# Winograd's form of Strassen's scheme for the last product of a two-layer expert network

## The chip, the cores and the metric

The kernel runs as one program on one core of a Trainium2 chip. Its time is the device time of one execution in microseconds; a comparison uses the median of several. Of the kernel before there are three runs: 1787.97, 1789.3 and 1793.09 us, median 1789.3. The engines are TensorE (PE; its weight loads are shown as PEld), VectorE (DVE), ScalarE (ACT), GpSimd (POOL) and SyncE (SP), whose queue issues all the transfers.

## The reference

Chunked attention, then two gated or activated expert layers on 4608 tokens of 512 numbers; everything is float32.

```python
scores = scale * np.matmul(q_c, k_c.transpose(0, 1, 2, 4, 3))      # chunks of 64
attn = softmax(scores)
x = np.matmul(attn, v_c)  # -> 4608 x 512
g = x @ w_gate;  x = (g * sigmoid(g) * (x @ w_val)) @ w_out        # layer 1, d_ff = 1536
h = x @ w_in                                                       # layer 2, d_ff = 2048
out = (h * sigmoid(1.702 * h)) @ w_out2
```

## The kernel before

A float32 product is done as three matmuls of the type fp32r: each operand is split into a high part (a cast on ScalarE or GpSimd) and a low part (a subtraction), and `mm3` (line 243) adds hi x hi, hi x lo and lo x hi in PSUM. `split` (line 239) makes the two parts.

The tokens are cut into 9 blocks of 512, the columns of a layer into tiles of 128. `passes` (line 252) has two passes per layer; a pass keeps its input weights in SBUF (the ring `w`, 21 tiles of 512 KB) and runs over all 9 blocks. A pass of the first layer has three groups of two column tiles of each of its two matrices, a pass of the second layer two groups of four column tiles.

The input products already use Winograd's form of Strassen's scheme: for each group `group_products` (line 526) computes seven products of 256 x 256 x 256 instead of eight, each of 12 matmuls with 256 columns, from seven combinations of the weights (`combos`, line 331, made ahead by `group_to_dram` and kept in DRAM as `wd_`) and seven of the tokens (`token_combos`, line 482, made by `x_to_dram` for the second layer). Two PSUM banks take them in turn, `ga` and `gb` or `s` and `a`; ScalarE and VectorE put the four quarters of the result together. `gated` (line 563) makes the activation h and its two parts.

The last product of a group is plain: `second` (line 582) multiplies the parts of h by an output weight tile (`od_`, loaded for each block in a ring `o` of three) into four sums of 512 columns, `ya` and `yb`, two banks each. These output steps (three matmuls of 512 columns; 16 per group in the second layer) are kept in the list `pend` and put between the products of the following group by `put` (line 690). `block_sum` (line 598) adds the sums of a pass: in the first pass of a layer they go to DRAM, in the last they are loaded again, added and, in the second layer, stored to the output.

All instructions are collected as operations with an engine, an estimated duration and a priority (`Program.op`, line 76), and `emit` (line 99) writes them out in the order of a planned run: at each step the engine that is free first takes the operation of lowest priority number among those that can begin. So each engine's order is fixed before the program runs. `spread` (line 664) puts the preparation of the next pass's weights (reading the 64-bit host words, combining, splitting, storing) over the pass before; GpSimd does the combining and splitting, with a ring `ws` of two tiles whose stores must land before a tile is used again.

## Time and profile before

| | |
|---|---|
| median of 3 runs | 1789.3 us |
| profiled execution | 1787.97 us, its span 1786.2 us |
| PE busy | 1736.1 us, 97% of the span, 13096 matmuls |
| DVE busy | 1068.7 us, 60% |
| ACT busy | 796.0 us, 45% |
| POOL busy | 489.9 us, 27% |
| DMA | 473.50 MB, 265 GB/s on average |
| PE on the chain that ended last | 90% of the span |

Busy time counts an engine as busy from the start to the end of each of its instructions; successive matmuls overlap in it, so a busy PE says only that matmuls follow closely, and the distance from one start to the next says how fast they run. The table is for the whole span; the stages differ and are read from stretches of it.

### The profile page before, as it was taken

What the parts mean: (1) busy time and instruction counts of PE and PEld (TensorE: products, weight loads), DVE (VectorE), ACT (ScalarE), POOL (GpSimd) and SP (SyncE); (2) the same over time, 40 slices, a digit from 0 to 9 for tenths busy, and PEclk for the clock granted to TensorE, in tenths of its full rate; (3) what the DMA queues carried; (4) which work ended last, traced back from release to release, by engine and by line L of the source; (5) the groups of instructions that cost most, each with busy time, mean ns of one, the idle gap of its engine ahead of it and who ended that gap; (6) DMA issues with size and microseconds to landing.
All of it is one profiled execution on the core that took longest, in us unless ns stands there. A gap on an engine that the chain in (4) does not pass through costs nothing.

```text
span 1786.2 us, 33210 instructions
## 1 busy us (share of the span) xinstructions
PE 1736.1 (97%) x13096; PEld 1579.0 (88%) x13096; DVE 1068.7 (60%) x1628; ACT 796.0 (45%) x1392; POOL 489.9 (27%) x542
## 2 busy tenths in 40 slices
PE   7779999999999999999999999999999999999998
PEld 6769998989899999999999998888888898888886
DVE  6787788778875467667666665333334444444444
ACT  5767666666663344444443354333333332322222
POOL 4664555455623144443353231000000000000000
PEclk8889999999999999999999999999999999999999
DMA  6567887788769988998889999766668666666664
GB/s 254 177 208 270 273 289 250 249 298 283 250 223 350 333 292 300 312 318 305 293 293 337 350 349 346 254 212 218 215 215 295 232 235 228 234 226 227 233 220 158
DMA packets 183915, 473.50 MB, mean 265 GB/s; under 512 B 19792, under 2 KB 46416, under 8 KB 183760
## 3 DMA queue, kind: packets, MB, share of 16 engines
q1 hardware_dynamic: 183760, 471.38, 76.4%
q8 instruction: 104, 1.70, 0.4%
q14 instruction: 51, 0.42, 0.1%
HBM read 336.56 MB, written 134.74 MB: 264 GB/s over the span
## 4 chain that ended last, share of the span: by engine, by line
PE 90%; DVE 4%; ACT 1%; issue 1%; POOL 0%; DMA 0%; DVEq 0%; ACTq 0%; SPq 0%; POOLq 0%
PE yb L244 6%; PE ya L245 6%; PE ya L244 6%; PE ya L246 6%; PE yb L246 6%; PE yb L245 6%; PE ga L244 6%; PE ga L246 6%; PE ga L245 6%; PE gb L244 4%; PE gb L246 4%; PE gb L245 4%; PE s L245 3%; PE s L246 3%; PE s L244 3%; PE a L246 2%
## 5 line engine op out<-in xcount | busy, mean ns | idle before, releaser
L237 DVE TENSOR_TENSOR h<-h,c 128x512 f32<-128x512 f32 x360 | 271.5, 768 | 39.2 <-ACT h L571 35.8
L244 PE MATMUL ga<-x,w 128*128 128x256 f32 x944 | 272.2, 288 | 19.1 <-ACT u L228 11.6
L571 ACT ACTIVATE h<-c 128x512 f32<-128x512 f32 x252 | 156.6, 632 | 274.9 <-DVE c L237 264.3
L246 PE MATMUL ga<-x,w 128*128 128x256 f32 x944 | 268.3, 284 | 0.7 <-POOL w L237 0.7
L245 PE MATMUL ga<-x,w 128*128 128x256 f32 x944 | 267.9, 284 | 0.0
L237 DVE TENSOR_TENSOR hl<-h,hh 128x512 fp32r<-128x512 f32 x252 | 187.6, 751 | 68.5 <-ACT hh L228 65.0
L228 ACT CAST hh<-h 128x512 fp32r<-128x512 f32 x252 | 155.8, 620 | 121.2 <-DVE h L237 72.8
L228 ACT COPY u<-ga 128x512 f32<-128x512 f32 x177 | 103.5, 585 | 235.5 <-PE ga L246 235.1
L237 DVE TENSOR_TENSOR c<-u,gb 128x512 f32<-128x512 f32 x177 | 121.0, 684 | 142.9 <-ACT u L228 107.4
L244 PEld LDWEIGHTS ga<-x,w 128*128 128x128 f32 x944 | 179.6, 190 | 29.4 <-ACT u L228 13.0
L244 PE MATMUL gb<-x,w 128*128 128x256 f32 x708 | 202.3, 286 | 0.0
L245 PE MATMUL gb<-x,w 128*128 128x256 f32 x708 | 201.0, 284 | 0.4 <-POOL x L237 0.4
L246 PE MATMUL gb<-x,w 128*128 128x256 f32 x708 | 201.3, 284 | 0.0
L245 PEld LDWEIGHTS ga<-x,w 128*128 128x128 f32 x944 | 179.9, 191 | 6.7
L246 PEld LDWEIGHTS ga<-x,w 128*128 128x128 f32 x944 | 179.8, 191 | 1.2 <-POOL w L237 1.2
L246 PE MATMUL s<-x,w 128*128 128x256 f32 x496 | 139.8, 282 | 0.0
L245 PE MATMUL s<-x,w 128*128 128x256 f32 x496 | 139.5, 281 | 0.0
L244 PE MATMUL s<-x,w 128*128 128x256 f32 x496 | 139.2, 281 | 0.0
L245 PEld LDWEIGHTS gb<-x,w 128*128 128x128 f32 x708 | 135.2, 191 | 4.0 <-POOL x L237 0.6
L244 PEld LDWEIGHTS gb<-x,w 128*128 128x128 f32 x708 | 135.2, 191 | 3.9
L246 PEld LDWEIGHTS gb<-x,w 128*128 128x128 f32 x708 | 135.1, 191 | 0.0
L237 DVE TENSOR_TENSOR c<-u,a 128x512 f32<-128x512 f32 x93 | 63.6, 684 | 117.7 <-ACT u L228 109.9
(144 smaller groups left out, 4223.8 us busy)
## 6 DMA issues: line engine op xcount, KB each, us to landing
x<-x_dram SPq DMA_DIRECT2D x189, 512.0 KB, 5.6
o<-od_b SPq DMA_DIRECT2D x144, 512.0 KB, 4.9
o<-od_a SPq DMA_DIRECT2D x102, 512.0 KB, 5.4
x_dram<-x SPq DMA_DIRECT2D x63, 512.0 KB, 4.6
wd_b<-ws SPq DMA_DIRECT2D x56, 256.0 KB, 5.2
w<-wd_b SPq DMA_DIRECT2D x28, 512.0 KB, 7.0
raw<-in_moe_w_out SPq DMA_DIRECT2D x56, 255.8 KB, 5.2
wd_a<-ws SPq DMA_DIRECT2D x42, 256.0 KB, 4.6
```

The costliest lines, as they stand in the source:

```text
L228: op("act", act_us(n), lambda: nc.scalar.copy(out=dst.ap, in_=cut(src.ap)), [src], [dst], prio)
L237: lambda: e.tensor_tensor(out=dst.ap, in0=of_a(a.ap), in1=of_b(b.ap), op=by), [a, b], [dst], prio)
L244: nc.tensor.matmul(o, ah, bh, start=first, stop=False, **kind)
L245: nc.tensor.matmul(o, ah, bl, start=False, stop=False, **kind)
L246: nc.tensor.matmul(o, al, bh, start=False, stop=last, **kind)
L571: op("act", act_us(512), lambda h=h, i=i, var=var, by=by: nc.scalar.activation(out=h.ap, in_=of(var)(c[i].ap), func=AF.Sigmoid, scale=by), ...
```

## The change

The second layer's last product is also computed with seven products instead of eight: the four quarters of a group's h (two halves of the columns, two halves of the tokens) are combined to seven operands, and so are the output weights. `group_gated` replaces `group_products` and `gated` for that layer: its seven input products all go into the bank `ga` in turn (some of them accumulate there), each is read by a copy or an add, and the gates and the seven operands follow, the operands in tiles of rings that the attention used. `last_product` is an output step for one of the seven labels and one half: six matmuls of 256 columns. The seven sums of a block stand in the seven other banks until `o_sum` combines them to four quarters. `out_combos` makes seven combinations of the output weights in the pass before; those of the first group stay in SBUF for a pass (`WO`, in the ring `w`), those of the second are loaded for each block. `x_to_dram` uses more buffers for the last block. In the first group of the layer three of the products have banks of their own. In the planner a product may follow its reader after 0.25 us (`near`), and a step of TensorE that depends on another follows it at once.

The core of the diff; a line of dots marks what is left out.

```diff
                     late = (0.3, 1.2)[a.eng == "pe" and o.eng != "pe"] + (1.5 if o.eng == "dma" else 0.0)
-                    a.done_at = max(a.done_at, end + (0.13 if a.eng == o.eng else late))
+                    if a.near and o.eng != "dma":
+                        late = 0.25
+                    a.done_at = max(a.done_at, end + ((0.0 if a.eng == "pe" else 0.13) if a.eng == o.eng else late))
...
+    GV, YS, OS = 1.42, 0.70, 0.714
+    ORDER = {1: "1265743", 2: "1675243", "o": "1245673"}
+    def step_us(g):
+        return 7 * GV + (4 * YS * len(g.fs) if g.layer == 1 else 14 * OS)
...
+        def of_pair(kind, tiles, made, name, done, order, var):
+            def fn(prio):
+                t0, t1 = [conv_tile((g.name, kind, var, i), tiles[i], prio) for i in range(2)]
+                for j, (m, src, cut) in enumerate(made(t0, t1, prio)):
+                    s = ring["ws"].new([P, 2, 256], F32R)
+                    hi, lo = [s.part(lambda ap, c=c: ap[:, c]) for c in range(2)]
+                    split(hi, lo, src, 256, prio + j, "pool", cut, "pool")
+                    i = order.index(m)
+                    store(done[i][0][:, i, var], s, [done[i][1].part(None)], prio + j)
...
+        if passes[p][0] == 2:
+            WO[gs[0]] = seven_load("w", gs[0], OD, [prio + (1 + i / 7) * step - 15 for i in range(7)])
...
+        for n, (m, src, cut) in enumerate(token_combos(xb, prio)):
+            i = ORDER[2].index(m)
+            pairs = ["qk", "ve"] if b < NB - 1 else ["qk", "ve", "tt", ("raw", "raw"), ("ws", "ws"), "hh", "te"]
+            hi, lo = [ring[t].new([P, 2, HT], F32R) for t in pairs[n % len(pairs)]]
+            split(hi, lo, src, 512, prio + n, "pool" if b < NB - 1 else ("dve", "pool")[n % 2], cut)
...
+    def group_gated(g, xs, at, put, early):
+        s1, u2, u3 = [ring["u"].new([P, 2, HT]) for _ in range(3)]
+        made = {}
+        hs = []
...
+        def gate(c, k, prio):
+            if not hs:
+                hs.append(ring["xr"].new([P, 4, 2, HT]))
+            h = hs[0].part(lambda ap: ap[:, k])
+            op("act", act_us(512), lambda: nc.scalar.activation(out=h.ap, in_=c.ap, func=AF.Sigmoid, scale=1.702),
+               [c], [h], prio, "sig")
+            tt(h, h, c, ALU.mult, 512, prio)
+            return h
+        def parts(label, src, prio, eng="dve"):
+            made[label] = [ring[t].new([P, 2, HT], F32R) for t in HOMES[label]]
+            split(*made[label], src, 512, prio, eng)
+        def follow(label, prio):
+            m = bank[label]
+            if label == "1":
+                copy(s1, m, 512, prio)
+            elif label == "6":
+                copy(u2, m, 512, prio)
+            elif label == "7":
+                copy(u3, m, 512, prio)
+                tt(u2, u2, u3, ALU.subtract, 512, prio, "pool")
+            elif label == "5":
+                c = quarter()
+                copy(c, m, 512, prio)
+                tt(u2, u2, c, ALU.add, 512, prio, "pool")
+                a["22"] = gate(c, 3, prio + 1)
+                parts("4", a["22"], prio + 3, "pool")
+            elif label == "2":
+                c = quarter()
+                tt(c, s1, m, ALU.add, 512, prio)
+                a["11"] = gate(c, 0, prio + 1)
+                parts("1", a["11"], prio + 2)
+            elif label == "4":
+                c = quarter()
+                tt(c, u3, m, ALU.subtract, 512, prio)
+                a["12"] = gate(c, 1, prio + 1)
+                parts("2", a["12"], prio + 3)
+            else:
+                c = quarter()
+                tt(c, u2, m, ALU.add, 512, prio)
+                a["21"] = gate(c, 2, prio + 1)
+        a = {}
+        alone = {"2": "gb", "3": "s", "4": "a"} if early else {}
+        z = ring["ga"].new([P, 2, HT])
+        bank = {label: ring[alone[label]].new([P, 2, HT]) if label in alone else z for label in ORDER[2]}
+        for i, label in enumerate("1263745" if early else ORDER[2]):
+            n = ORDER[2].index(label)
+            product(bank[label], W[g][n], xs[n], label in "675", at(i), True)
+            if label != "3" or not early:
+                follow(label, at(i))
+            if i == 6:
+                if early:
+                    follow("3", at(i))
+                prio = at(i)
+                tt(a["22"], a["21"], a["22"], ALU.add, 512, prio + 1)
+                parts("5", a["22"], prio + 2)
+                tt(a["21"], a["11"], a["21"], ALU.subtract, 512, prio + 2)
+                tt(a["11"], a["22"], a["11"], ALU.subtract, 512, prio + 2)
+                parts("6", a["11"], prio + 3)
+                parts("7", a["21"], prio + 4)
+                tt(a["12"], a["12"], a["11"], ALU.subtract, 512, prio + 4)
+                parts("3", a["12"], prio + 5)
+            put(i)
+        return made
...
+    def last_product(bank, label, w, parts, var, first, last, prio):
+        hi, lo = parts
         def fn():
-            if layer == 1:
-                mm3(ys[e].ap, w.ap[:, 0, es], w.ap[:, 1, es], hh.ap, hl.ap, first, last)
+            for t in range(2):
+                ts = slice(t * P, (t + 1) * P)
+                mm3(bank.ap[:, t], hi.ap[:, var, ts], lo.ap[:, var, ts], w.ap[:, var, 0], w.ap[:, var, 1],
+                    first and t == 0, last, skip_group_check=True)
+        op("pe", OS, fn, [w, hi, lo], [bank], prio)
...
+    def o_banks():
+        ya, yb = [ring["y" + i].new([P, 2, 2, 256]) for i in "ab"]
+        one = [ring[t].new([P, 2, 256]) for t in ("gb", "s", "a")]
+        two = [t.part(lambda ap, i=i: ap[:, i]) for t in (ya, yb) for i in range(2)]
+        return dict(zip("1245673", two + one))
...
+        m = banks[label]
+        if label == "1":
+            kept["s"] = ring["e"].new([P, 2, 256])
+            copy(kept["s"], m, 512, prio)
+        elif label == "2":
+            c = part_of(0, "yv")
+            if final:
+                tt(c, c, kept["s"], ALU.add, 512, prio, "pool")
+                tt(c, c, m, ALU.add, 512, prio)
+            else:
+                tt(c, kept["s"], m, ALU.add, 512, prio)
+            out_quarter(0, c)
+        elif label == "6":
+            tt(kept["s"], kept["s"], m, ALU.add, 512, prio)
+        elif label == "7":
+            u2, u3 = kept["s"], ring["e"].new([P, 2, 256])
+            tt(u3, u2, m, ALU.add, 512, prio)
+            c = part_of(3, "yv")
+            if final:
+                tt(c, c, u3, ALU.add, 512, prio, "pool")
+                tt(c, c, banks["5"], ALU.add, 512, prio)
+            else:
+                tt(c, u3, banks["5"], ALU.add, 512, prio)
+            out_quarter(3, c)
+            tt(u3, u3, banks["4"], ALU.subtract, 512, prio)
+            if final:
+                c = part_of(2, "t")
+                tt(c, c, u3, ALU.add, 512, prio, "pool")
+                u3 = c
+            out_quarter(2, u3)
+            tt(u2, u2, banks["5"], ALU.add, 512, prio)
+        elif label == "3":
+            u4 = kept["s"]
+            tt(u4, u4, m, ALU.add, 512, prio)
+            if final:
+                c = part_of(1, "t")
+                tt(c, c, u4, ALU.add, 512, prio, "pool")
+                u4 = c
+            out_quarter(1, u4)
...
+                after_first = p and passes[p - 1][0] < layer and b == j == 0
+                def put(i, tj=tj, n=n, step=step, layer=layer, after_first=after_first):
+                    left = n * (7 - i - (i > 3)) // 8 if layer == 1 else 0 if after_first else n * (6 - i) // 7
+                    while len(pend) > left:
+                        pend.pop(0)(tj + (i + (i > 4) + 0.5 + (n - len(pend) if after_first else 0)) * step / 8)
...
```

## Rows read from the trace of the kernel before

**Rows 1.** Stretches: PE, PEld, DVE, ACT, POOL busy us (instructions), PEclk, DMA share, GB/s.

```profile
0.00:545.00 545.00, 504.35 (x5098) 458.42 (x5099) 432.08 (x674) 353.77 (x612) 287.93 (x329) 0.96 0.74 253
545.00:1013.00 468.00, 467.30 (x3242) 435.17 (x3241) 301.91 (x440) 190.13 (x342) 175.61 (x182) 1.00 0.91 315
1013.00:1393.00 380.00, 380.00 (x2387) 341.66 (x2386) 171.15 (x263) 137.08 (x241) 26.35 (x32) 1.00 0.77 264
1393.00:1777.00 384.00, 384.00 (x2375) 343.71 (x2374) 161.84 (x251) 115.05 (x199) 0.00 (x0) 1.00 0.64 223
sum 1786.20, PE 1736.12 PEld 1579.01 DVE 1068.67 ACT 796.03 POOL 489.89; mean PE 347.22 PEld 315.80 DVE 213.73 ACT 159.21 POOL 97.98
```

**Rows 2.** Timeline of TensorE in the second layer: start, duration, instruction.

```profile
1203.94 0.28 PE L244 MATMUL gb<-x,w 128*128 128x256 f32 x1
...
1205.36 0.39 PE L244 MATMUL yb<-o,hh 128*128 128x512 f32 x1
...
1206.76 0.28 PE L244 MATMUL ga<-x,w 128*128 128x256 f32 x1
```

**Rows 3.** Timeline of VectorE: the same instruction in two successive blocks.

```profile
1459.69 0.69 DVE L237 TENSOR_TENSOR c<-u,gb 128x512 f32<-128x512 f32 x1 [3.50 <-ACT u L228]
...
1501.99 0.69 DVE L237 TENSOR_TENSOR c<-u,gb 128x512 f32<-128x512 f32 x1 [3.47 <-ACT u L228]
```

**Rows 4.** Timelines of TensorE, ScalarE and VectorE around hand-offs of a bank.

```profile
1201.05 0.28 PE L246 MATMUL ga<-x,w 128*128 128x256 f32 x1
1201.37 0.59 ACT L228 COPY u<-ga 128x512 f32<-128x512 f32 x1 [2.03 <-PE ga L246]
...
128.45 0.67 DVE L237 TENSOR_TENSOR c<-u,ga 128x512 f32<-128x512 f32 x1
129.18 0.39 PE L244 MATMUL ga<-x,w 128*128 128x256 f32 x1 [0.97 <-DVE c L237]
```

**Rows 5.** Groups of instructions, 1400 to 1750 us: count, busy, mean ns, idle before.

```profile
L237 DVE TENSOR_TENSOR h<-h,c 128x512 f32<-128x512 f32 x68 | 46.1, 687 | 11.6 <-ACT h L571 10.8
...
L237 DVE TENSOR_TENSOR c<-u,gb 128x512 f32<-128x512 f32 x25 | 17.2, 689 | 41.0 <-ACT u L228 31.0 <-PE gb L246 10.0
```

**Rows 6.** The same groups, 1000 to 1100 us, GpSimd at work.

```profile
L237 DVE TENSOR_TENSOR h<-h,c 128x512 f32<-128x512 f32 x24 | 18.6, 789 | 3.3 <-ACT h L571 3.2
...
L237 DVE TENSOR_TENSOR c<-u,gb 128x512 f32<-128x512 f32 x8 | 5.5, 684 | 8.2 <-ACT u L228 5.3 <-ACT raw L321 2.8
```

**Rows 7.** Timelines of VectorE and GpSimd: the first layer's last block.

```profile
1031.44 0.69 DVE L237 TENSOR_TENSOR xr<-yv,yb 128x512 f32<-128x512 f32 x1 [0.30 <-DMA yv<-y_dram]
...
1056.69 1.29 POOL L237 TENSOR_TENSOR k<-xr,q 128x512 fp32r<-128x512 f32 x1 [4.31 <-DMA x_dram<-k]
```

**Rows 8.** Stretches of full and of steady transfers.

```profile
1060.00:1130.00 70.00, 70.00 (x437) 62.72 (x436) 34.22 (x55) 28.18 (x52) 12.31 (x20) 1.00 0.98 348
1400.00:1750.00 350.00, 350.00 (x2191) 314.42 (x2190) 150.99 (x234) 107.36 (x186) 0.00 (x0) 1.00 0.66 232
```

**Rows 9.** Timeline of GpSimd: a cast that waited for a store, its subtraction.

```profile
1082.37 0.40 POOL L230 CAST ws<-t 128x256 fp32r<-128x256 f32 x1 [7.87 <-DMA od_b<-ws]
1082.85 0.74 POOL L237 TENSOR_TENSOR ws<-t,ws 128x256 fp32r<-128x256 f32 x1
```

**Rows 10.** Timelines at the end: TensorE, VectorE, the queue of SP.

```profile
1777.09 0.39 PE L246 MATMUL yb<-o,hl 128*128 128x512 f32 x1
...
1781.72 1.28 DVE L237 TENSOR_TENSOR yv<-yv,yb 128x512 f32<-128x512 f32 x2 [4.31 <-DMA yv<-o_dram]
1782.44 0.93 SPq L224 DMA_DIRECT2D out<-yv  x2
```

**Rows 11.** Timeline of TensorE after a long idle time.

```profile
72.41 0.58 PE L244 MATMUL ga<-x,w 128*128 128x256 f32 x1 [4.42 <-ACT u L228]
```

**Rows 12.** Stretches behind that idle time.

```profile
72.40:75.00 2.60, 2.59 (x12) 2.60 (x13) 2.60 (x4) 1.90 (x5) 2.60 (x3) 0.50 0.53 199
75.00:79.00 4.00, 4.00 (x14) 3.23 (x14) 3.89 (x7) 3.96 (x6) 1.78 (x2) 0.59 0.19 44
```

More of the change, by code (lines that the diff above doesn't have):

```diff
@@ L66 @@
 class Op:
-    __slots__ = ("eng", "us", "fn", "prio", "deps", "follows", "table", "n", "done_at")
+    __slots__ = ("eng", "us", "fn", "prio", "deps", "follows", "table", "near", "n", "done_at")
 class Program:
@@ L280, in attention_two_moe_kernel @@
             start[p].append(t)
-            t += sum(7 * GV + 4 * YS * len(g.fs) for g in gs) + (13.0 if p == 0 and b < NB - 1 else 0)
+            t += sum(step_us(g) for g in gs) + (13.0 if p == 0 and b < NB - 1 else 0)
     start.append([t])
@@ L534, in group_products @@
         for i, (k, goes_on) in enumerate(((0, 0), (1, 0), (0, 1), (1, 0), (0, 1), (0, 0), (1, 1))):
[L535 to L546 removed]
+            m, at_i = bank[k], at(i)
+            product(m, W[g][i], xs[i], goes_on, at_i)
             if i == 0:
@@ new lines, in attention_two_moe_kernel, with quarter @@
+    HOMES = {"1": ("hh", "hl"), "2": ("hh", "hl"), "4": ("hh", "hl"), "5": ("h", "h"), "6": ("q", "k"), "7": ("v", "xt"),
+             "3": ("xt", "xt")}
+    def group_gated(g, xs, at, put, early):
+        s1, u2, u3 = [ring["u"].new([P, 2, HT]) for _ in range(3)]
+        made = {}
+        hs = []
+        quarters = []
+        def quarter():
+            if not quarters:
+                c = ring["c"].new([P, 2, 2, HT])
+                quarters.extend(c.part(lambda ap, k=k: ap[:, k]) for k in range(2))
+            return quarters.pop(0)
+        def gate(c, k, prio):
[60 more added lines that the diff above has]
+            put(i)
+        return made
@@ L594, in attention_two_moe_kernel @@
     y_dram = pool["dram"].tile([P, KD, NT], F32, name="y_dram")
-    o_dram = pool["dram"].tile([P, KD, NT], F32, name="o_dram")
+    o_dram = pool["dram"].tile([P, NB, 4, 512], F32, name="o_dram")
+    od2 = {}
     yd = {}
     def block_sum(p, b, ys, e, prio):
-        layer = passes[p][0]
-        first = p == 0 or passes[p - 1][0] != layer
-        last = p == NPASS - 1 or passes[p + 1][0] != layer
-        dram = (y_dram if layer == 1 else o_dram)[:, e, b * BT:(b + 1) * BT]
-        if first:
-            s = ring["yv"].new([P, BT])
+        dram = y_dram[:, e, b * BT:(b + 1) * BT]
+        s = ring["yv"].new([P, BT])
+        if p == 0:
@@ L606, in block_sum @@
             copy(s, ys[e], 512, prio, "act" if e % 2 else "dve")
-            yd[layer, b, e] = Buf(None)
-            store(dram, s, [yd[layer, b, e]], prio)
+            yd[b, e] = Buf(None)
+            store(dram, s, [yd[b, e]], prio)
             return
-        s = ring["yv"].new([P, BT])
-        load(s, dram, prio - 14, [yd[layer, b, e]])
-        if last and layer == 1:
-            if e == 0:
-                xr[b] = ring["xr"].new([P, KD, BT])
-            tt(xr[b].part(lambda ap: ap[:, e]), s, ys[e], ALU.add, 512, prio)
-            if e == KD - 1:
-                x_to_dram(xr.pop(b), b, prio + 3)
-            return
@@ L619, in block_sum @@
-        tt(s, s, ys[e], ALU.add, 512, prio)
-        if last:
-            t0 = b * BT + e * P
-            store(out[t0:t0 + P, :], s, [], prio)
-        else:
-            yd[layer, b, e] = Buf(None)
-            store(dram, s, [yd[layer, b, e]], prio)
+        load(s, dram, prio - 14, [yd[b, e]])
+        if e == 0:
+            xr[b] = ring["xr"].new([P, KD, BT])
+        tt(xr[b].part(lambda ap: ap[:, e]), s, ys[e], ALU.add, 512, prio)
+        if e == KD - 1:
+            x_to_dram(xr.pop(b), b, prio + 3)
@@ L683, in attention_two_moe_kernel @@
             xs = X.pop((p, b))
[L684 removed]
             for j, g in enumerate(gs):
[L686 removed]
+                step = step_us(g)
                 tj = t + j * step
                 n = len(pend)
[L690 to L715 removed]
```

216 lines of the change are left out of this document (128 added, 88 removed).

## The prediction

> **What bounds the kernel now.** The page's busy line comes first: TensorE is busy for 1736 of 1786 us, VectorE for 1069. That is an average over stages, so the next view is the table of stretches. It shows the attention stage with the first pass of the first layer (to about 545 us, TensorE idle for 40 us of it), the second pass (0.7 us idle), the two passes of the second layer (busy 380.00 of 380 and 384.00 of 384 us), and then a tail of 9.2 us in which TensorE has stopped [rows 1]. The change touches the second layer, and there nothing ends a wait of TensorE, so only three things can change the time: the length of TensorE's own stream, new waits in it, and the tail. That the busy time is dense work and not overlapping records is seen in the timeline: inside a product of 12 matmuls of 256 columns one starts every 0.118 us (1203.94 to 1205.36, 1.42 us for 12), and six matmuls of 512 columns follow one another in 1.40 us, 0.233 us each [rows 2]. The granted clock is 1.00, which is the 2.4 GHz level [rows 1].
>
> One group of four column tiles is then 7 products of 12 short matmuls and 16 output steps of 3 long ones: 84 x 0.118 + 48 x 0.233 = 9.94 + 11.20 = 21.14 us; a block of two groups should take 42.28. The same VectorE instruction returns after 42.30 us in successive blocks [rows 3]. So the stage is accounted for without a gap.
>
> **TensorE's stream.** The 48 long matmuls of a group become 7 labels x 2 halves x 2 token tiles x 3 = 84 short ones. At the spacing of the products, which also load a weight tile for each matmul, they take 84 x 0.118 = 9.94 us. The group loses 1.26 us, and 36 groups (two passes, nine blocks, two groups) lose **45.4 us**. The bounds on that are narrow, since the shape (128x256, its own weight load) is the one already measured: with the planner's own 0.714 us for six matmuls it would be 43.3.
>
> **The hand-off of the one product bank.** Today the products alternate between banks. Now all seven of a group go through one bank, so each waits until ScalarE or VectorE has read the one before. Rows on both sides of that hand-off exist. ScalarE starts its copy 0.32 us after the start of the last matmul (1201.05 to 1201.37), and the copy takes 0.59 us; VectorE's add from PSUM takes 0.67 to 0.69; TensorE, when it waits for one, starts 0.06 us after its end (128.45 + 0.67 to 129.18) [rows 4, 5]. From the start of the last matmul to the next product that is 0.97 us by ScalarE and 1.07 by VectorE, if VectorE starts as soon as ScalarE does. The two output steps queued between two products cover 1.42 us plus the matmul's own 0.12, so 0.6 and 0.5 us are left over. An uncovered hand-off costs 0.85 us (0.97 less the 0.12 that the next matmul would have taken anyway).
>
> What can use up the slack is work in front of the reader. Per group ScalarE now has 15 instructions of about 0.6 us (9 of 20 us) and VectorE 17; with the seven of the block's sums 41 per block, spaced 0.61 us where two follow each other (two in 1.28) [rows 10]: 25 of 39.8 us, 63% instead of 43% [rows 8]. An instruction that has just begun holds the reader for at most 0.6 us, which the slack nearly covers. Beside GpSimd VectorE is slower: in 1000 to 1100 us, with GpSimd at work, h<-h,c took 789 ns, against 687 later without it, while the add from PSUM (c<-u,gb) kept 684 against 689 [rows 5, 6]. The new kernel gives GpSimd three instructions of 512 elements, 1.3 us each [rows 7], in every group, so this comes back in part. I take 0.1 us per group, **+4 us** (between 0 and 0.5 per group, 18 us).
>
> By the Trainium skill (Perfetto Trace Analysis, Optimizing Tensor Performance) independent matmul groups should rotate through different PSUM banks, and larger matmuls are more efficient than smaller ones. Both speak against this change. On the second half the rows agree only faintly: 256 columns cost 0.118 us in the short form and 0.117 in the long. The first half, taken at its worst, is the second rival below.
>
> **First boundary, at about 1013 us.** The gates of the second layer now write a tile of the ring xr, which has one buffer, and the last block of the first layer holds that buffer until x_to_dram has split it. Before, its last sum came at 1031.44, its last split on GpSimd at 1056.69, after 4.31 us of waiting for a store [rows 7]: 26 us for the splitting. The new buffer pairs of the last block take these store waits away, and every other split goes to VectorE; four sums and four splits at 0.6 are some 5 us. In that time TensorE has the second group's products, but no output steps to put between them: four hand-offs at 0.85 are 3.4 us, and some 3 more until the first parts are made. I take **+6 us**; 0 if the sums come earlier, 20 if the buffer is freed as late as today.
>
> **Second boundary, at about 1370 us.** Of the 21 buffers w the second layer used 14; now the first group's seven output weights stay in the other seven, and nothing of the next pass can be loaded until the last block frees them. Around the boundary, in some 60 us, 21 weight tiles, 14 input tiles and 7 output tiles of 512 KB and 2 MB of sums must pass: 24 MB, 400 GB/s. The rows show 348 GB/s at a DMA share of 0.98, and 232 at 0.66 in steady state [rows 8]. 24 MB at 348 GB/s take 69 us, so up to 9 us are missing; I take **+4 us** (0 to 9).
>
> **What hides.** Making the output weights takes GpSimd, per group, 6 more pairs of a cast (0.40) and a subtraction (0.74) and 8 more sums of about 0.74 us [rows 9]: 13 us, 26 per pass, in stretches where it is busy for 176 of 468 us and for 26 of 380; in the last pass it has nothing left to do [rows 1], so the work was ready well ahead. Output weights loaded: 8 tiles per block before, 7 now. If this cover goes, GpSimd's queue is what is late (third rival). In the first layer only the planner's constant for a step that follows another on TensorE changes; its second pass has 0.7 us to lose or win, and I put the reordering at 0 (up to 5 us either way).
>
> **The tail.** TensorE's last matmul starts at 1777.09; then two loads of old sums wait for their buffers, VectorE adds at 1781.72, the last stores are issued from 1782.44, and the span ends at 1786.2, 9.1 us later [rows 10]. Afterwards the four old quarters have four buffers, so the loads are done early, and behind the last matmul stand 0.4 us to the reader, an add on VectorE (0.69), one on GpSimd (1.3) and a store as now (3.3 from the second store's issue to the end, the two issues taking 0.93): 5.7. **-3 us** (between -5 and 0). The gate chain of the last group ends about 8.5 us after its last product by durations of 0.6 to 0.7 us an instruction, and the output steps ahead of its last label last 10, so it should not wait there.
>
> **Sum.** The profiled execution took 1788.0 us (span 1786.2): 1788.0 - 45.4 + 4 + 6 + 4 - 3 = 1753.6. The median of the runs is 1.3 us above the profiled one, so **1755 us**.
>
> **Rivals.**
> 1. *No new wait*: only the stream and the tail count. 1788.0 - 45.4 - 3 + 1.3 = 1741. For it: the slack of the hand-off and the planner's order. Against it: both boundaries lack a buffer.
> 2. *The gain turns into bubbles at the one bank.* 252 products at 0.85 us each would be 214 us and a kernel at 1955. By the Trainium skill's rule on rotating banks, above, it would go this way. The slack of 0.5 us speaks against it; but if 41 of the 252 are uncovered (one in six), the gain of 34 us is gone and the time stays near 1789.
> 3. *GpSimd's queue*, the slower side. Today TensorE needs nothing from GpSimd in the second layer. Now the adds that make u2, and a part of a22, stand in its queue behind the weight preparation for the next pass, and its casts wait for stores: 7.87 us before the one at 1082.37, the longest such wait of that stretch [rows 9]. From the fourth product to the read of the seventh are three slots of 2.85 us, less a copy and an add of 2 us: 6.5 us of slack. A hold of 7.9 us costs 1.4 us and the reader behind it a hand-off of 0.85; with the 56 stores of one pass, at 1.2 us each on average, 67 us, less what is saved: 1822. It decides from 0.6 us per store on. Against it: the long holds came where GpSimd had little else to do, and DMA was full (0.98) only until 1130 us [rows 8].
> 4. *The clock.* After 4.42 us of idle [rows 11] TensorE's clock was 0.50 (the 1.2 GHz level) from 72.4 to 75 us and 0.59 for 4 us more [rows 12]: half of 2.6 and 0.41 of 4 are 2.9 us lost. Twelve such drops would eat the gain; one in each group costs 104 us, 1859 us. Bubbles of 0.85 us are far below that idle time, and in the first 545 us, with 40 us of idle in it, the mean clock was still 0.96 [rows 1]. The Trainium skill (TensorE: Matmul & The Clock Gate, "A second HAM failure mode") does tell of a kernel that cycles PSUM banks and loses its clock to frequent small idles. No stretch of the second layer shows it yet.
>
> **Chances.** The forecast, with waits somewhat below or far above my 14 us (1746 to 1784): 0.67. The first rival 0.15, the second 0.07, the third 0.08, the fourth 0.03. About 0.3% (5 us) is what a measurement of this kernel tells from no change. Faster: 0.67 + 0.15 = 0.82; within 0.3%: 0.07; slower: 0.11. From 1741 to 1784 lie the forecast and nearly all of the first rival, 0.8.
>
> **What would show it.** In the new profile the block period in the second layer should be near 40 us (42.30 now), with 168 short matmuls per group at 0.118 us and no bubble before most products; VectorE near 63% there; gaps of TensorE only at the two boundaries, a few us each; about 6 us behind the last matmul. It is wrong if gaps stand before products in every block with ScalarE or VectorE as releaser (second rival), if VectorE's add for the last product waits for GpSimd (third), or if the clock of a second-layer stretch is below 1.00 (fourth).

## The result, and the profile after

The changed kernel takes 1806.4 us (median of four, 1805.4 to 1806.7) against 1789.5 us of the kernel before on the same chip: ratio 1.0091, 95% interval 1.0073 to 1.0108. It is slower by 17 us, where 34 us less were forecast. The table of stretches, with the columns of [rows 1], cut at 545, 1013 and 1393 us as there:

```profile
545.00:1013.00 468.00, 467.77 (x3243) 435.52 (x3242) 272.09 (x396) 167.49 (x296) 135.66 (x131) 1.00 0.84 291
1013.00:1393.00 380.00, 357.59 (x2853) 348.55 (x2852) 306.96 (x425) 191.06 (x338) 189.42 (x199) 0.98 0.85 286
1393.00:1797.00 404.00, 391.68 (x3218) 384.47 (x3217) 286.28 (x394) 174.54 (x294) 123.99 (x91) 1.00 0.72 233
```

The first layer is as it was (its last output step starts at 1028.7, before at 1027.7). In the second layer TensorE, which had no idle time in [rows 1], is idle for 22 us of 380 and for 12 of 404. VectorE has 306.96 us of work there in place of 171, GpSimd 189 in place of 26.

The stream itself did become shorter. VectorE's timeline, the same instruction in successive blocks, twice late in the layer's first pass (pass 1) and twice in its last pass:

```profile
1322.39 0.69 DVE L241 TENSOR_TENSOR c<-u,ga 128x512 f32<-128x512 f32 x1 [0.56 <-PE ga L250]
...
1363.17 0.69 DVE L241 TENSOR_TENSOR c<-u,ga 128x512 f32<-128x512 f32 x1 [0.56 <-PE ga L250]
...
1444.70 0.69 DVE L241 TENSOR_TENSOR c<-u,ga 128x512 f32<-128x512 f32 x1 [0.56 <-PE ga L250]
...
1486.65 0.69 DVE L241 TENSOR_TENSOR c<-u,ga 128x512 f32<-128x512 f32 x1 [0.56 <-PE ga L250]
```

The block takes 40.78 us in the one and 41.95 in the other; it took 42.30 [rows 3]. Taking from TensorE's timeline every distance between matmul starts beyond 0.1185 us gives the waits (with what half clock adds to the distances): 0.8 us in a quiet block of pass 1, 2.1 in one of the last pass, none in the kernel before. From the last output step of layer 1 on, the first six stretches up to that VectorE instruction in successive blocks (to 1281 us) hold 8.8, 13.6, 5.0, 2.4, 2.4 and 3.5 us, and the end of the stream 4.3. The list of TensorE's waits (engine, line and releaser: us, times, longest), 1028 to 1055 us, and then 1055 to 1108:

```profile
PE ga L248 <- ACT u L232: 2.1, 3, 0.7
PE ga L248 <- DVE c L241: 1.8, 1, 1.8
PE ya L248 <- ACT hh L232: 1.7, 1, 1.7
PE ga L248 <- ACT c L232: 0.7, 1, 0.7
PE ya L250 <- DVE hl L241: 0.5, 1, 0.5
```

```profile
PE ga L248 <- ACT u L232: 3.1, 2, 1.9
PE yb L248 <- DMA o<-od_b: 1.7, 1, 1.7
PE ga L248 <- DVE c L241: 1.6, 2, 1.2
PE ya L248 <- ACT hh L232: 0.7, 1, 0.7
```

In the second list a hand-off is late by up to 1.9 us, not by the bare 0.85: the reader itself began late. And there the clock fell. Stretches of the same columns:

```profile
1028.00:1055.00 27.00, 20.20 (x151) 18.51 (x150) 20.94 (x29) 13.58 (x26) 11.17 (x7) 1.00 0.96 353
1055.00:1062.00 7.00, 5.17 (x42) 4.79 (x41) 4.50 (x7) 3.78 (x7) 4.28 (x5) 1.00 0.99 334
1062.00:1070.00 8.00, 7.32 (x38) 6.80 (x37) 7.00 (x11) 4.79 (x11) 4.64 (x5) 0.57 0.84 314
1070.00:1075.00 5.00, 2.69 (x21) 2.27 (x19) 5.00 (x6) 3.43 (x7) 3.46 (x4) 1.00 0.72 228
1075.00:1080.00 5.00, 4.22 (x22) 4.22 (x23) 2.85 (x6) 2.37 (x5) 4.04 (x6) 0.66 0.72 238
...
1123.00:1128.00 5.00, 5.00 (x32) 5.00 (x31) 3.58 (x5) 2.30 (x4) 2.67 (x3) 0.66 0.60 215
```

TensorE had been busy for 20.2 of 27 and 5.2 of 7 us when the mean fell to 0.57, near the 1.2 GHz level. Ahead of the third fall it had waited 2.2 us for one copy (to 1122.51). By the means 0.43 x 8 + 0.34 x 5 + 0.34 x 5 = 6.8 us at most went there; the distances between matmul starts that grew from 0.12 to 0.21 us add up to 5.2.

The preparation of the last pass's weights is in another place. Stores of prepared weights in the kernel before, 750 to 1010 us and 1010 to 1300 us (count, KB, median us to landing):

```profile
wd_b<-ws SPq DMA_DIRECT2D x18, 256.0 KB, 5.5
od_b<-ws SPq DMA_DIRECT2D x8, 256.0 KB, 6.7
...
od_b<-ws SPq DMA_DIRECT2D x8, 256.0 KB, 5.8
wd_b<-ws SPq DMA_DIRECT2D x6, 256.0 KB, 6.1
```

and in the changed one:

```profile
od_b<-ws SPq DMA_DIRECT2D x2, 256.0 KB, 5.8
...
wd_b<-ws SPq DMA_DIRECT2D x28, 256.0 KB, 4.6
od_b<-ws SPq DMA_DIRECT2D x28, 256.0 KB, 4.4
```

All 56 stores of a pass now fall behind 1010 us. The split of the first layer's last block takes tiles of the rings t, raw and ws; the preparation needs the same rings and is written later in the program, so in the planned order it stands behind that split.

In the last pass the timeline shows most of what makes a block 1.2 us longer than in pass 1 (GpSimd, VectorE, ScalarE, TensorE):

```profile
1512.53 3.39 POOL L241 TENSOR_TENSOR t<-t,e 128x512 f32<-128x512 f32 x2 [2.03 <-DVE e L241]
1512.98 0.68 DVE L241 TENSOR_TENSOR e<-e,a 128x512 f32<-128x512 f32 x1
1513.57 3.63 DVE L241 TENSOR_TENSOR xr<-xr 128x512 f32<-128x512 f32 x3
1516.51 0.62 ACT L232 CAST v<-xr 128x512 fp32r<-128x512 f32 x1 [1.09 <-DVE xr L241]
1517.23 0.62 ACT L232 CAST q<-xr 128x512 fp32r<-128x512 f32 x1
1517.76 0.58 ACT L232 COPY u<-ga 128x512 f32<-128x512 f32 x1
1518.39 0.38 PE L248 MATMUL ga<-x,w 128*128 128x256 f32 x1 [0.55 <-ACT u L232]
```

While GpSimd makes its two final adds, three VectorE instructions take 1.21 us each (0.69 in e1, where VectorE makes those adds); the casts wait for them, and the copy of the product bank stands behind the casts in ScalarE's fixed order.

The tail: TensorE's last matmul starts at 1797.67, the span ends at 1803.6, 5.9 us later.

### The profile page after: what moved, and what is told of

Read it like the earlier page. It is cut to its first block, busy times and chain, and to the rows that moved or that the text cites. A ratio compares the mean times of both kernels' runs of the same rounds, so it can differ in the third digit from the quotient of the medians.

```text
span 1803.6 us, 36622 instructions
## 1 busy us (share of the span) xinstructions
PE 1718.8 (95%) x14392; PEld 1623.1 (90%) x14392; DVE 1302.3 (72%) x1884; ACT 883.6 (49%) x1536; POOL 751.5 (42%) x762
## 4 chain that ended last, share of the span: by engine, by line
PE 72%; DVE 14%; issue 3%; ACT 3%; DMA 2%; POOL 1%; SPq 0%; POOLq 0%; DVEq 0%; ACTq 0%
PE ga L248 9%; PE ga L250 8%; PE ga L249 8%; DVE xr L241 4%; PE yb L248 4%; PE gb L248 4%; PE yb L250 4%; PE yb L249 4%; PE gb L250 4%; PE gb L249 4%; PE ya L249 3%; PE ya L248 3%; PE ya L250 3%; PE s L248 2%; PE s L250 2%
## 5 line engine op out<-in xcount | busy, mean ns | idle before, releaser
L248 PE MATMUL ga<-x,w 128*128 128x256 f32 x1652 | 480.1, 291 | 44.3 <-ACT u L232 29.7
L250 PE MATMUL ga<-x,w 128*128 128x256 f32 x1652 | 468.2, 283 | 1.0 <-POOL w L241 1.0
L249 PE MATMUL ga<-x,w 128*128 128x256 f32 x1652 | 467.4, 283 | 0.0
L248 PEld LDWEIGHTS ga<-x,w 128*128 128x128 f32 x1652 | 313.8, 190 | 65.3 <-ACT u L232 37.9
L249 PEld LDWEIGHTS ga<-x,w 128*128 128x128 f32 x1652 | 314.0, 190 | 4.1
L250 PEld LDWEIGHTS ga<-x,w 128*128 128x128 f32 x1652 | 313.9, 190 | 1.5 <-POOL w L241 1.5
L241 DVE TENSOR_TENSOR xr<-xr,c 128x512 f32<-128x512 f32 x144 | 129.6, 902 | 103.9 <-ACT xr L650 99.8
L241 DVE TENSOR_TENSOR h<-h,c 128x512 f32<-128x512 f32 x216 | 167.6, 792 | 12.6 <-ACT h L612 10.9
L241 DVE TENSOR_TENSOR c<-u,ga 128x512 f32<-128x512 f32 x146 | 99.9, 684 | 68.0 <-PE ga L250 66.2
L248 PE MATMUL gb<-x,w 128*128 128x256 f32 x496 | 143.0, 288 | 1.1 <-DVE c L241 1.1
L249 PE MATMUL gb<-x,w 128*128 128x256 f32 x496 | 141.4, 285 | 1.1 <-POOL x L241 1.1
L250 PE MATMUL gb<-x,w 128*128 128x256 f32 x496 | 141.7, 286 | 0.0
L612 ACT ACTIVATE h<-c 128x512 f32<-128x512 f32 x108 | 68.2, 633 | 121.1 <-DVE c L241 120.7
L241 DVE TENSOR_TENSOR xr<-xr 128x512 f32<-128x512 f32 x144 | 118.9, 825 | 4.2 <-POOL hl L241 0.6
L650 ACT ACTIVATE xr<-c 128x512 f32<-128x512 f32 x144 | 90.7, 632 | 58.3 <-DVE c L241 52.7
L241 POOL TENSOR_TENSOR k<-xr,q 128x512 fp32r<-128x512 f32 x24 | 41.4, 1724 | 156.6 <-DVE xt L241 89.4
L248 PEld LDWEIGHTS gb<-x,w 128*128 128x128 f32 x496 | 95.3, 192 | 4.2 <-DVE c L241 1.3
```

What stands on the lines that cost most here:

```text
L241: lambda: e.tensor_tensor(out=dst.ap, in0=of_a(a.ap), in1=of_b(b.ap), op=by), [a, b], [dst], prio)
L248: nc.tensor.matmul(o, ah, bh, start=first, stop=False, **kind)
L249: nc.tensor.matmul(o, ah, bl, start=False, stop=False, **kind)
L250: nc.tensor.matmul(o, al, bh, start=False, stop=last, **kind)
L612: op("act", act_us(512), lambda h=h, i=i: nc.scalar.activation(out=h.ap, in_=of(0)(c[i].ap), func=AF.Sigmoid), [c[i]], [h], prio, "sig")
L650: op("act", act_us(512), lambda: nc.scalar.activation(out=h.ap, in_=c.ap, func=AF.Sigmoid, scale=1.702), [c], [h], prio, "sig")
```

## The experiments

Time from layer 1's last output step to TensorE's last matmul, from each profile: before 749.4 us, changed 769.0. It is given with each run, since layer 1 itself ended between 1025.9 and 1036.7 us in these profiles (below). It is one profile each time: up to 1390 us e1 has the changed kernel's order of instructions on every engine, yet its first six stretches hold 33.0 us of waits where the changed kernel's hold 35.7, so up to 3 us there say nothing. The first eight runs have one execution each, beside the kernel before at 1788.5 (e1 to e4) and 1790.5 us (e5, e6, e7, e9).

**e1_final_dve.** The four final adds of the last pass go from GpSimd to VectorE.

```diff
-                tt(c, c, kept["s"], ALU.add, 512, prio, "pool")
+                tt(c, c, kept["s"], ALU.add, 512, prio)
...
```

> The four adds of old sums that each block of the last pass gives to GpSimd go to VectorE; nothing else is changed. Theory A (GpSimd's reads hold VectorE's sums of two SBUF tiles, the casts behind them stand in ScalarE's queue in front of the copy of the product bank, and TensorE waits for that copy): the block of the last pass falls from 42.0 to about 40.8 us, as in the end of the pass before, and the kernel from 1806 to about 1796. Rival B (VectorE has too much to do by itself): four more adds are 2.4 us per block on VectorE, so the block stays at 42 or grows, and the kernel takes 1806 to 1815.

1797.8 us, 759.3 behind layer 1; blocks of the last pass 41.13 in place of 42.03. Groups of the last pass, 1400 to 1750 us (count, busy, mean ns, idle before), first of the changed kernel, then of this one:

```profile
L241 DVE TENSOR_TENSOR xr<-xr 128x512 f32<-128x512 f32 x68 | 57.1, 840 | 2.1
L241 DVE TENSOR_TENSOR c<-u,ga 128x512 f32<-128x512 f32 x51 | 35.1, 688 | 20.5 <-PE ga L250 19.5
```

```profile
L241 DVE TENSOR_TENSOR xr<-xr 128x512 f32<-128x512 f32 x68 | 46.7, 687 | 1.6
L241 DVE TENSOR_TENSOR c<-u,ga 128x512 f32<-128x512 f32 x52 | 35.7, 687 | 20.8 <-PE ga L250 19.7
```

The sums that stood beside GpSimd's adds, both operands in SBUF, fall from 840 to 687 ns; those with a PSUM operand stay. The Trainium skill states (SBUF — State Buffer, "Who interferes with whom") that GpSimd's ports are VectorE's second pair, held by one at a time. The trace agrees. VectorE as a whole is busier (259.6 us in place of 250.0), and the subtraction k<-xr,q, also of two SBUF tiles, is now slower (1106 ns on average in place of 681), but no wait of TensorE for the product bank is left in the list. 0.9 of a block's 2.1 us of waits in the last pass came from GpSimd's adds: 7.5 us in the pass. The rest of the 9.7 us behind layer 1 lies at the first boundary, within the scatter named above; e5 and e6, and e10 and e11, which differ by this edit, differ by 6.8 and 6.9 us. What stays in this kernel, 1400 to 1750 us, is another wait, of 0.7 us per block:

```profile
PE ya L248 <- ACT e L232: 4.7, 7, 0.7
```

The output step of label 2 waits for the copy of label 1's sum: both lie in the tile ya.

**e2_strict.** TensorE's planned order kept nearer to the priorities, so that two output steps stand between products.

```diff
...
-s <= first + (0.1 if eng == "dve" else 0.3)
+s <= first + (0.1 if eng == "dve" else 3.2 if eng == "pe" and o.prio > strict_from else 0.3)
...
```

> In the second layer the planner takes TensorE's steps by priority even if the one of lowest number can begin only up to 3.2 us later; so in the first pass of the layer two output steps stand before nearly every product, where the changed kernel has places with one and with four. Theory C (a hand-off with one output step before it lacks cover: 1.07 us against 0.71 + 0.12): the last blocks of that pass fall from 40.77 to 40.1 us, the last pass by about as much, 1806 to about 1794. Rival D (the reader is late by itself, whatever stands before the product): blocks within 0.2 us of before, 1806.

1806.1 us, 772.0 behind layer 1; blocks of 41.4 and 42.26, no shorter than 40.77 and 42.03. The wait on the copy in ya, 0.84 us in each block, took the place of what the order saved: in 1400 to 1750 us TensorE's waits for the product bank fall from 6.8 to 3.8 us. What the places with a single output step cost by themselves this run does not tell; e9 parts the two sums as well.

**e3_no_prep.** The last pass reuses pass 2's weights, and nothing is prepared during pass 2 (the output is then that of other weights).

```diff
+        if p == 2:
+            for g, g2 in zip(passes[3][1], passes[2][1]):
+                WD[g], OD[g] = WD[g2], OD[g2]
+            return []
```

> The preparation of the last pass's weights is left out (that pass takes those of the pass before, so its part of the output is another); GpSimd, VectorE, ScalarE and the transfers have that much less to do between 1010 and 1300 us. Theory E (the preparation costs TensorE's waits in that stretch): the blocks between 1155 and 1281 fall from 42.3 and 41.3 to 40.8 us, and of the 27 us of waits from 1010 to 1155 some 10 go: 1806 to about 1791. Rival F (those first waits come from the buffer xr that the last block of the first layer holds): only the 5 us of the blocks after 1155 go, 1801.

1781.9 us, 746.5 behind layer 1: 22.5 less than the changed kernel. The stretch 1013 to 1393 us:

```profile
1013.00:1393.00 380.00, 370.99 (x3034) 364.10 (x3033) 261.81 (x380) 172.23 (x291) 76.23 (x59) 1.00 0.76 248
```

TensorE's idle time there falls from 22 to 9 us and the clock stays at 1.00. Waits by stretch: 8.8, 1.4, and 0.8 from then on. The transfers of the preparation are gone as well as its instructions; of the changed kernel's waits from 1010 to 1396 us a transfer ended 1.7 us.

**e4_no_last_split.** The last block of layer 1 is not combined and split; layer 2 reads the block before it twice (the last block's output is then another).

```diff
-            x_to_dram(xr.pop(b), b, prio + 3)
+            x = xr.pop(b)
+            if b < NB - 1:
+                x_to_dram(x, b, prio + 3)
```

> The last block of the first layer is summed but not combined and split for the second layer (which reads the block before it in its place, so the last block's output is another); the buffer xr is free as soon as the sums are made. Theory F (that buffer holds the first gates of the second layer): the waits from 1010 to 1108 us fall from 22 to about 6, 1806 to about 1790. Rival E (weight preparation and transfers make them): only some 3 us go, 1803.

1784.1 us, 744.6 behind layer 1. With the split gone its rings are free, and 31 stores are back at 750 to 1010 us:

```profile
1013.00:1393.00 380.00, 372.81 (x3047) 365.80 (x3045) 277.60 (x392) 177.20 (x303) 121.53 (x115) 1.00 0.80 264
```

Either one taken away gives back some 23 us, though the other stays. With the split alone (e3) the first six stretches hold 8.6 us beyond 0.8 each, with the preparation alone (e4) 7.0, with both 30.9: the loss is in their meeting.

**e5_own_rings and e6_own_dve.** The split of the last block goes through three pairs of buffers that the preparation does not use; e6 has e1's edit as well.

```diff
...
-["qk", "ve", "tt", ("raw", "raw"), ("ws", "ws"), "hh", "te"]
+["qk", "ve", "hh"]
...
```

> The changed kernel with one line altered: the last block of the first layer splits into the rings q, k, v, e and h alone, no longer into t, raw and ws, which the weight preparation also takes, in the order in which both are written down. Theory G (through those rings the preparation of the last pass's weights had to stand behind the last block's split, so it ran beside the second layer, whose readers it delays): stores of that preparation appear again between 750 and 1010 us (about 30, 2 in the changed kernel), all blocks from the second on take 40.8 us in the first pass of the layer, and the kernel 1806 - 24 = about 1782, as without preparation and without the split. Rival H (the preparation moved for another reason, and the extra buffers were needed for the split): the stores stay behind 1010 us and the first boundary grows by some 5 us, 1806 to 1812.

> Both at once: the last block's split in rings of its own, and the four adds of old sums on VectorE. Theories A and G act at different times, so their gains should add: 1782 less 9, about 1773, with blocks of 40.8 us in the first and 41.1 in the second pass of the layer. If the first gain comes from less work on GpSimd in general, the second would shrink: 1778 or more.

e5: 1794.6 us, 758.7 behind layer 1; e6: 1787.1 and 751.9. The preparation is back (30 stores between 750 and 1010 us, 26 behind), but only 10.3 of the 24 us expected are won; the rest is lost again at the boundary. Longest waits of e5, 1025 to 1110 us:

```profile
PE ya L248 <- ACT hh L232: 10.5, 1, 10.5
PE ga L248 <- ACT u L232: 2.4, 4, 0.7
```

and what ScalarE does meanwhile:

```profile
1040.08 0.62 ACT L232 CAST q<-xt 128x512 fp32r<-128x512 f32 x1 [2.84 <-DMA x_dram<-q]
1043.27 0.62 ACT L232 CAST v<-xr 128x512 fp32r<-128x512 f32 x1 [2.57 <-DMA x_dram<-v]
1045.81 0.62 ACT L232 CAST h<-xt 128x512 fp32r<-128x512 f32 x1 [1.93 <-DMA x_dram<-h]
1048.34 0.62 ACT L232 CAST q<-xr 128x512 fp32r<-128x512 f32 x1 [1.91 <-DMA x_dram<-q]
```

With few buffers the casts wait for stores, and the first gates follow at 1049.8.

**e7_before_rings.** The kernel before with only the seven pairs of buffers and every other split on VectorE.

```diff
-            hi, lo = [ring[t].new([P, 2, HT], F32R) for t in (("q", "k"), ("v", "e"))[i % 2]]
-            split(hi, lo, src, 512, prio + i, "pool", cut)
+            pairs = ["qk", "ve"] if b < NB - 1 else ["qk", "ve", "tt", ("raw", "raw"), ("ws", "ws"), "hh", "te"]
+            hi, lo = [ring[t].new([P, 2, HT], F32R) for t in pairs[i % len(pairs)]]
+            split(hi, lo, src, 512, prio + i, "pool" if b < NB - 1 else ("dve", "pool")[i % 2], cut)
```

> The kernel before with one part of the change alone: the last block of the first layer splits into the seven pairs of buffers (t, raw, ws, h among them), every other split on VectorE. Theory G: the preparation of the last pass's weights moves behind 1010 us here too (some 35 of its 44 stores), but in this kernel TensorE needs nothing from GpSimd in the second layer and reads each bank with more slack, so the time stays within 0.3% of 1788.5. Rival I (preparation that late costs time by itself, through transfers or VectorE): more than 5 us slower.

1800.6 us, 761.7 behind layer 1 (749.4 before). The preparation moves behind 1010 us here too (no store from 750 to 1010), yet TensorE then has no wait from 1100 to 1400 us: the old loop covers it. The 12 us are one place, where the gate's parts need the tiles h that the split holds, and half clock behind it (the wait, then the stretch):

```profile
PE ya L244 <- ACT hh L228: 8.3, 1, 8.3
```

```profile
1048.00:1055.00 7.00, 6.40 (x15) 4.78 (x16) 5.60 (x11) 4.50 (x9) 1.53 (x2) 0.52 1.00 353
```

So after the boundary the late preparation costs nothing beside the old loop, where beside the new one the stretches from 1108 to 1281 us hold 10 us of waits beyond 0.8 each.

**e9_pairs_strict.** e6 with e2's order, and labels 1 and 4 (not 1 and 2) in the tile ya.

```diff
-        return dict(zip("1245673", two + one))
+        return dict(zip("1425673", two + one))
...
```

> As the one before it, with two things more: TensorE's steps in strict order of priority, and the sums of labels 1 and 4 share a tile, 2 and 5 another (before 1 and 2, 4 and 5). Theory J (in the strict run the output step of label 2 waited 0.84 us per block for the copy of label 1, since both sums lie in one tile of two banks; with that gone the strict order gives every hand-off its two output steps): blocks of 40.0 to 40.2 us in both passes and about 1773 - 14 = 1759. Rival D (the readers are late whatever the order): blocks as without, 40.8 and 41.1 us, 1773.

1792.6 us, 752.1 behind layer 1. The last pass's blocks are the shortest of all, 40.64 us, with this wait left in 1400 to 1750 us:

```profile
PE ya L248 <- DVE e L241: 3.4, 7, 0.5
```

4 us won there (41.16 us a block in e6) are lost at the first boundary, where the first three stretches hold 27.5 us in place of e6's 23.1. Order and pairing were changed together, so the 4 us are not divided between them.

**e10_free_rings and e11_free_dve.** As the changed kernel, but the last block's split uses seven pairs that the preparation does not use (q and k twice, v and e, three in ring o, the two h); e11 has e1's edit as well.

```diff
+            pairs = ["qk", "ve"] if b < NB - 1 else ["qk", "ve", "o", "o", "o", "hh", "qk"]
+            if pairs[n % len(pairs)] == "o":
+                both = ring["o"].new([P, 2, 2, HT], F32R)
+                hi, lo = [both.part(lambda ap, c=c, both=both: ap[:, c]) for c in range(2)]
...
```

> The changed kernel, only the buffers of the last block's split replaced: seven pairs that neither the weight preparation nor a pending store holds (q and k, v and e, three tiles of ring o, the two h, then q and k again). Theory J (what the first boundary lost is the order of buffers alone: with t, raw and ws the preparation is pushed behind it, with only three pairs the splits wait for stores): preparation stores back at 750-1010 us, TensorE waits about 9 us in the stretch 1010-1055, about 2 in the next two blocks together, then 0.8 per block; last pass unchanged at 42.0 per block; time about 1785 (20 below the changed kernel). Rival K (the first boundary costs 17 us of waits whenever the preparation runs before it, since GpSimd and ScalarE are then behind with layer 1's own work): waits of 17 us in 1010-1060 and a time about 1794, as with three pairs.

> The same buffers, and the four final adds of the last pass on VectorE in place of GpSimd. If the two causes add up: 9 us less in the last pass (41.1 per block in place of 42.0), so about 1776 by theory J and about 1786 by rival K; the kernel before stands at about 1789. If they do not add up (the last pass then waits for something else), the last pass stays near 42.

e10: 1799.8 us, ratio 1.0051 (1.0036 to 1.0065), 758.8 behind layer 1; e11: 1793.9, 1.0016 (1.0006 to 1.0026), 751.9. Behind layer 1 both equal e5 and e6. The 20 us that theory J of e10 expected did not come: the long wait is gone, but the waits of the first three stretches are 9.9, 9.4 and 4.0 in place of 17.6, 3.6 and 1.7, the same 23 us. Yet the buffers of e10 were not free. Layer 2's own operands go to h, q and k, and SyncE issues the second store of q only at 1061.31, after 6.1 us of waiting for stores from the tiles o. Casts of operands into h and q wait for those stores, and the copy of the product bank stands behind the second (ScalarE, then TensorE):

```profile
1061.57 0.62 ACT L232 CAST h<-xr 128x512 fp32r<-128x512 f32 x1 [3.54 <-DMA x_dram<-h]
1067.31 0.62 ACT L232 CAST q<-xr 128x512 fp32r<-128x512 f32 x1 [5.12 <-DMA x_dram<-q]
1067.84 0.58 ACT L232 COPY u<-ga 128x512 f32<-128x512 f32 x1
1068.47 0.58 PE L248 MATMUL ga<-x,w 128*128 128x256 f32 x1 [2.59 <-ACT u L232]
```

So theory J is not settled by this run.

**e12_held and e13_held_own.** e11 and e6, with the last three of the eight preparation jobs held back in the planned order until layer 2's third block.

```diff
+                    if p == 2 and len(jobs) < 3:
+                        prog.hold = products[28]
                     job(at + 10)
+                    prog.hold = None
...
```

> The kernel with the free buffers and the final adds on VectorE; the last three of the eight preparation jobs for the last pass (21 of 56 stores) are held back in the planned order until the third block of layer 2 begins. Theory L (the preparation's rest and the split of the last block share ScalarE, VectorE and GpSimd at the first boundary; alone each is covered): the first two segments' TensorE waits fall from 9.0 and 8.7 to about 9 and 2, later ones with preparation rise to at most 2.5 per block for three blocks; from layer 1's last output step to the end 745 us in place of 752, time about 1783 to 1787. Rival M (the waits come from the order of layer 2's own first blocks, the preparation only happens to lie there): unchanged, 752 us behind layer 1 and a time of 1790 to 1794.

> The same hold on the kernel whose last block is split through three pairs. Theory L: the waits of 17.9 in the first segment (the splits wait for stores) stay or fall by a third, those of the next two blocks (3.1 and 1.9) fall to 1.5 and 0.8; 745 to 750 us behind layer 1, time about 1782 to 1786. Rival M: 752 us and 1787.

e12: 1787.0 us, ratio 0.9992 (0.998 to 1.0005), 749.4 behind layer 1; e13: 1789.3, 1.0012 (1.0002 to 1.0023), 751.9. In e13 the second and third stretch fall from 3.1 and 1.9 to 1.2 and 1.1 us, as theory L has it, and the two to which the preparation moved rise from 1.3 and 0.8 to 2.0 and 2.4: nothing is won. e12 wins 2.5 of the 7 us expected; its first two stretches keep 10.4 and 7.0 us. Its casts into h and q wait 2.7 and 4.9 us for stores as in e10. Its longest waits, 1025 to 1110 us:

```profile
PE ga L250 <- ACT u L234: 5.4, 5, 1.9
PE ga L250 <- DVE c L243: 2.0, 1, 2.0
```

**e14_own_dve_again.** e6 once more.

> The kernel with three pairs and the final adds on VectorE once more, to have an interval for it: it had 1787.1 against 1790.5 of the kernel before. If layer 1, whose instructions are the same in the kernels with three pairs and with free buffers, ends at a time that belongs to the program, it ends again near 1026 us and the time is 1787; if it changes from one execution to the next, its end and the time spread by up to 8 us.

1789.2 us (12 executions, 1787.6 to 1795.8), ratio 1.0008 (0.9995 to 1.0021); layer 1 ended at 1026.8, 751.9 behind it. The profiled ends agree to 0.6 us, but the time spreads by 8 us from one execution to the next; the single 1787.1 of e6 was a low one. No variant that does the whole work beats the kernel before by what can be measured; the nearest, e12, equals it.

## Why the prediction was wrong

From layer 1's last output step to TensorE's last matmul, and around it:

| term | forecast | measured | from |
|---|---|---|---|
| stream | -45.4 | -40.4 | 769.0 less 60.0 of waits, against 749.4 |
| one product bank | +4 | +24.8 | ten stretches of 0.8, eight blocks of 2.1 |
| first boundary, with the preparation behind it | +6 | +30.9 | six stretches, less 0.8 each |
| second boundary | +4 | 0 | its blocks hold 0.8 like the quiet ones |
| end of the stream | 0 | +4.3 | behind the last full block |
| tail | -3 | -3.2 | 5.9 us, 9.1 before |
| layer 1 | 0 | +1.0 | its last output step |
| sum | -34 | +17.4 | spans: 1803.6 - 1786.2 |

**Right:** the tail, and the sign and nearly the size of the stream. The second boundary's 4 us did not come, though the range (0 to 9) allowed for that; that the end of the stream cost as much is luck, and makes no forecast right. A quiet block is 40.77 - 0.8 = 39.97 us of matmuls, 0.119 us each for 336 of them; at 0.118 I had taken the better end, and the planner's 43.3 was nearer. The bare hand-off was also right: the first stretch has four, of 0.84 to 0.89 us beyond a matmul's spacing, 3.4 us as forecast.

**The step that failed first** is "the work was ready well ahead". It was ready because its rings were free. The prediction counted the preparation's instructions on GpSimd and praised the last block's new buffers for ending store waits, but did not ask who else takes t, raw and ws: the order of allocation puts the whole preparation of the last pass behind that split. By e3 and e4 this is worth 22.5 and 24.4 us, of the 25 by which the first boundary exceeded its term; without the preparation (e3) the boundary holds 8.6 us where 6 were forecast. By e5 and e10 10 of these come back when the rings are separate. Of the other 12 (e5 or e10 against e3), e5 has 9 in the first stretch, where the split's casts wait for stores, and e10 8 in the second, where layer 2's casts wait for the split's stores. Holding the preparation's rest back gains nothing in e13 and 2.5 us in e12. How the 12 divide between buffers and that rest stays open.

**The second** is "I take 0.1 us per group" for the one bank. Slack of 0.5 us is there when the reader's engine is free at once. It was priced with one instruction of 0.6 us in front of the reader, and with three instructions per group on GpSimd; the four final adds of each block of the last pass were left out of that count. The trace shows a chain: GpSimd beside VectorE, VectorE beside a cast, and the cast ahead of the copy in ScalarE's order. e1 removes 7.5 us by untying the first link, and most of what then stands in a block, 0.7 us, is the wait for the copy in ya, not one for the product bank. The bound of 18 us was 7 short; VectorE's share in the last pass is 250 of 350 us, 71% and not 63, because instructions with two SBUF operands grew: beyond 687 ns each xr<-xr (68 at 840), xr<-xr,c (68 at 867) and h<-xr,h (17 at 1006) take 28 us more, 8% of the 350. [rows 5, 6] had shown the effect.

**A smaller one** is "it should not wait there", of the end of the stream. The gate chain held it for 0.6 us; the loads of the output weights did so for 2.8 (of TensorE's waits of the changed kernel, 1396 us to the end):

```profile
PE a L248 <- DMA o<-od_b: 1.7, 1, 1.7
PE yb L248 <- DMA o<-od_b: 0.8, 1, 0.8
```

**The rivals.** The second (bubbles at the one bank) had the place of 25 us right. The rule that the Trainium skill gives for it (Perfetto Trace Analysis, Optimizing Tensor Performance) agrees in direction. The third came true in part, and by another path: the preparation with its 56 stores cost 22.5 us (e3), 0.4 per store, where 0.6 alone would have eaten the gain. In the lists of VectorE's and ScalarE's waits from 1055 to 1285 us none ends with GpSimd. VectorE is busy for 202 of those 230 us, and five of the six late copies of the product bank there stand in ScalarE's order behind a cast xt<-xr that waited 0.7 to 1.5 us for VectorE. The fourth came true in three places: some 5 us of half clock behind the first boundary's waits. The prediction had ruled it out by the length of a single bubble; here no single one was over 2.2 us. In e3 the first stretch has the same waits (8.8 us), and the clock stays at 1.00: what tips it these runs do not settle.

**Open:** how the 10 to 13 us that remain at the first boundary in e10 to e13 divide between buffers, the preparation's rest and half clock; no run gives the split buffers that nothing else needs. Half clock is the smaller part: the grown distances between matmul starts add up to 4.7, 1.1, 3.0 and 1.3 us in these four. e10 and e11, with the same order there and mean clocks of 0.92 and 0.98 from 1025 to 1110 us, hold 23.3 and 21.9 us in the first three stretches: 3.6 us more of half clock made them 1.4 us longer.

## What to carry to other kernels

Where a scheme shortens TensorE's stream but passes one bank from product to reader to product, the slack of the hand-off must be set against chains of the other engines' work, not against one instruction. And a change that lends buffers of one stage to another moves whatever next needs them: go through each ring by who allocates from it next, before calling work hidden.

## What the runs showed that was not expected

- VectorE's instructions with two SBUF operands went from 0.69 to 1.21 us beside GpSimd's adds, those with a PSUM operand kept 0.69.
- Layer 1 ended at 1026.2 us in e6 and at 1033.0 in e9, with the same order of instructions on every engine up to there. Its cause is open; a difference below 8 us between single executions of this kernel says little, unless it is read behind layer 1's end, where e6 and e14 agree and the first boundary of e1 and the changed kernel differs by 3 us.
